# Retention ahead of two feed-forward networks on one core: state products in four quarters of the array, five unit buffers, nine early weight slices

## The chip, the cores and the metric

The kernel runs on one core of one Trainium2 chip. The metric is the device time of one execution in microseconds. Three executions of the kernel before took 1071.54, 1073.75 and 1075.57 us; their median is 1073.75 us.

## What is computed

Retention over 4 sequences of 768 tokens with 8 heads of 64 features, and on its output, 3072 tokens of 512 features, two feed-forward networks of width 2048, all in float32:

```python
for t in range(S):
    state = gamma[None, :, None, None] * state + np.einsum('bhd,bhe->bhde', k[:, :, t], v[:, :, t])
    y[:, :, t] = scale * np.einsum('bhd,bhde->bhe', q[:, :, t], state)
x = np.ascontiguousarray(y.transpose(0, 2, 1, 3)).reshape(B * S, H * D)
h = x @ w_in
x = (h * (1.0 / (1.0 + np.exp(-1.702 * h)))) @ w_out
r = np.maximum(x @ w_in2, 0.0)
out = (r * r) @ w_out2
```

## The kernel before

The work has two parts on PE. The first 106 us are the **retention stage**: 24 units (4 sequences of 6 pieces of 128 tokens), each with all 8 heads. The rest are the two networks, in blocks of tokens, with float32 values split into a high and a low float32r part so that each product takes three matmuls. The first network's first block of 512 tokens (`n == 0` of the loop at line 719) runs in 16 steps `f` of 24 matmuls.

A **unit** is one tile of 128x2048 (1 MB: q and k transposed in pairs of heads, then k and v by tokens). It is loaded by two DMAs on SP's queue (`load_unit`, line 444) into one of `UNITS` buffers. In step `u` of the loop at line 563 the program issues, in this order:

- `scores(u)`: eight matmuls of 64 rows give k times q for each head (line 459, tile `sc`, two banks, two buffers). The two heads of a pair lie in the upper and lower half of the partitions, so they use different row halves of the array. Then v is scaled (`vs`), on POOL for the first six units and each third one (line 478), on ACT otherwise (line 483).
- `split_0()`: for the first four units the output of two steps ago is split into the network's operands, by four casts on ACT (line 494) and four subtractions on DVE (line 495).
- `outputs(u - 1)`: eight matmuls of 64 columns multiply the masked scores `pt` by `vs` into `yp` (line 508); eight of 64x64 outputs add k times v to the sequence's state in PSUM, `dp` (line 518); ACT copies that state to SBUF (line 525), as two blocks of 64x64 per pair on the diagonal of a 128x128 tile whose other blocks were filled with zeros once (line 431); and four matmuls of 128x128 add the state up to the unit before, times q, to `yp` (line 529), in all units but the first of a sequence.
- `cv_step(...)`: on DVE the mask of unit `u` (line 468, `masked`) and the scaling of the output of unit `u - 1` (lines 542, 546, 549, `scaled`), and between them, where `u` is in `CVU`, the conversion of one **weight slice** of the first network. A slice is 512 KB; it is loaded from POOL's queue into one of five `raw` buffers (`cv_load`, line 109), rescaled by two ACT operations (lines 124, 125; `cv_a`, up to two slices ahead), joined by three DVE operations (lines 129, 134, 142), and one step later split by a cast on ACT (line 157) and a subtraction on DVE (line 162). There are 32 slices; those not made in this stage are made in the steps `f` of the first block (lines 608 to 611). `cv["ahead"]` says how many slices may be loaded ahead.
- `load_unit(u + UNITS - 1)` on SP, into the buffer of unit `u - 1`.

Every engine works through its instructions in the order in which the program issued them. SP also lets each DMA wait for the landing of the one eight of its DMAs earlier. Behind the loop the pools of this stage are closed, and the network starts with `up(0, 0)` (line 594).

Of the kernel before, what the change touches and what calls it, by code (L numbers as in the profile page):

```python
# [10 lines left out]
F32 = mybir.dt.float32  # L11
# [19 lines left out]
WA = 8  # L31
LOOK = 2
WARM = 10
UNITS = 4
XHELD = 4
NL = NT // (2 * TB)
NQ = NF // 2
# [4 lines left out]
SLOTS = 8  # L42
EARLY = 2
BG = 4.8
CVU = (6, 8, 10, 12, 14, 16, 18, 20, 21, 22, 23)
RAWS = 5
BGUP = 1.8

# [9 lines left out]
def tile_retention_then_two_ffns(  # L58
# [10 lines left out]
    nc = tc.nc  # L69
    v = nc.vector  # L70
# [13 lines left out]
    xout = {j: keep_p.tile([P, KD, TB], F32, tag=f"xo{j}", name=f"xout{j}") for j in range(XHELD, NT // TB)}  # L84
# [310 lines left out]
    xs = {}  # L395
# [14 lines left out]
    with tc.manual_schedule():  # L410

        with (
# [13 lines left out]
            table_sb = att.tile([P, 1], F32, tag="table", name="table_sb", bufs=1)  # L426
            nc.scalar.activation(out=table_sb, in_=warm_sb[:, 0:1], func=ACTF.Gelu_apprx_sigmoid)

            st_sb = [att.tile([P, NP, P], F32, tag=f"st{i}", name=f"st{i}", bufs=1) for i in range(2)]
            for t in st_sb:  # L430
                nc.gpsimd.memset(t, 0.0)
            hl[0] = hl_tiles(0)
            cv["pool"] = att


            warm = aps.tile([P, 2, NP, P], F32, tag="sc", name="warm")
# [15 lines left out]
            def scores(u):  # L452
                t = units[u]
                qk = t[:, 0:1024].rearrange("p (b n a i) -> p b n a i", b=2, n=2, a=2)
                v = t[:, 1536:2048].rearrange("p (h e) -> p h e", h=H)
                sc = aps.tile([P, 2, NP, P], F32, tag="sc", name=f"sc{u}")
                for p in range(NP):
                    for r in range(2):
                        nc.tensor.matmul(  # L459
                            sc[:, r, p, :],  # L460
                            qk[64 * r:64 * r + 64, p // 2, 1, p % 2, :],
                            qk[64 * r:64 * r + 64, p // 2, 0, p % 2, :],
                            start=True, stop=True,
                        )
                pt = att.tile([P, 2, NP, P], F32, tag="pt", name=f"pt{u}")

                def masked():
                    nc.vector.tensor_tensor(
                        out=pt.rearrange("p r a i -> p (r a) i"),
                        in0=sc.rearrange("p r a i -> p (r a) i"),  # L470
                        in1=mask_sb.unsqueeze(1).to_broadcast([P, H, P]),
                        op=ALU.mult,
                    )

                vs = att.tile([P, H, D], F32, tag="vs", name=f"vs{u}")
                if u < CPB or u % 3 == 0:

                    nc.gpsimd.tensor_tensor(
                        out=vs, in0=v, in1=vtab_sb[:, u % CPB, :].unsqueeze(2).to_broadcast([P, H, D]), op=ALU.mult
                    )  # L480
                else:
                    for h in range(H):
                        nc.scalar.mul(vs[:, h, :], v[:, h, :], vtab_sb[:, u % CPB, h:h + 1])
                pend[u] = (pt, vs)
                return masked

            def split_0():
# [4 lines left out]
                for k in range(KD):  # L492
# [3 lines left out]
                        out=lo[:, cols], in0=xt[:, k, :], in1=hi[:, cols], op=ALU.subtract  # L496
                    )

            def outputs(u):
                t = units.pop(u)  # L500
                pt, vs = pend.pop(u)
                b, c = divmod(u, CPB)
                qk = t[:, 0:1024].rearrange("p (b n a i) -> p b n a i", b=2, n=2, a=2)
                kn = t[:, 1024:1536].rearrange("p (h e) -> p h e", h=H)
                yp = aps.tile([P, NP, P], F32, tag="yp", name=f"yp{u}")
                for p in range(NP):
                    for r in range(2):
                        nc.tensor.matmul(  # L508
                            yp[64 * r:64 * r + 64, p, :], vs[:, 2 * p + r, :], pt[:, r, p, :],
                            start=(p == 0), stop=(c == 0), skip_group_check=True,  # L510
                        )
                dp, st = state.pop(b, (None, None))
                if c == 0:
                    dp = aps.tile([P, 2, NP, D], F32, tag="dp", name=f"dp{b}")
                if c < CPB - 1:
                    for p in range(NP):
                        for r in range(2):
                            nc.tensor.matmul(
                                dp[64 * r:64 * r + 64, 0, p, :], kn[:, 2 * p + r, :], vs[:, 2 * p + r, :],
                                start=(c == 0 and p == 0), stop=(c == CPB - 2), skip_group_check=True,  # L520
                            )
                    ns = st_sb[u % 2]
                    for r in range(2):
                        h = slice(64 * r, 64 * r + 64)
                        nc.scalar.copy(out=ns[h, :, h], in_=dp[h, 0])
                    state[b] = (dp, ns)
                if c > 0:
                    for p in range(NP):
                        nc.tensor.matmul(  # L529
                            yp[:, p, :], st[:, p, :], qk[:, p // 2, 0, p % 2, :],  # L530
                            start=False, stop=True, skip_group_check=True,
                        )
                j, o = divmod(u, UPB)
                cols = slice(o * P, (o + 1) * P)
                if 0 < j < XHELD and o == 0:
                    xs[j] = block_tiles(f"x{j}")

                def scaled():
                    if 0 < j < XHELD:
                        for i in range(2):  # L540
                            pair = slice(2 * i, 2 * i + 2)
                            v.tensor_tensor(
                                out=xs[j][i][:, :, cols], in0=yp[:, pair], in1=ytab_sb[c][:, pair], op=ALU.mult
                            )
                    elif j > 0:
                        v.tensor_tensor(out=xout[j][:, :, cols], in0=yp, in1=ytab_sb[c], op=ALU.mult)
                    else:
                        xt = att.tile([P, NP, P], F32, tag="x0", name=f"x0_{u}")
                        v.tensor_tensor(out=xt, in0=yp, in1=ytab_sb[c], op=ALU.mult)
                        pend["x"] = (xt, cols)  # L550

                return scaled
# [10 lines left out]
            for u in range(NU + 1):  # L563
                masked = scores(u) if u < NU else None
                split_0()
                scaled = outputs(u - 1) if u > 0 else None
                if 0 < u < CPB:
                    for p in range(NP):
                        nc.scalar.mul(ytab_sb[u][:, p, :], ytab_sb[0][:, p, :], ystep_sb[:, u, p:p + 1])
                if u == 16:  # L570
                    cv["ahead"] = RAWS
                cv_step(2 * WA if u in CVU else 0, masked, scaled, u >= 4)
                if u > 0:
                    load_unit(u + UNITS - 1)

# [13 lines left out]
        def up(n, f):  # L589
            hi, lo = weights(f, 0)  # L590
            hp = hp_p.tile([P, TB], F32, tag="h", name=f"h{n}_{f}")
            for k in range(KD):
                xh, xl = hl[n][k]
                nc.tensor.matmul(hp, lo[:, k], xh, start=(k == 0), stop=False)  # L594
                nc.tensor.matmul(hp, hi[:, k], xh, start=False, stop=False)  # L595
                nc.tensor.matmul(hp, hi[:, k], xl, start=False, stop=(k == KD - 1))  # L596
            g = g_p.tile([P, TB], F32, tag="gs", name=f"gs{n}_{f}", bufs=1)
            gh = g_p.tile([P, TB], F32R, tag="gh", name=f"gh{n}_{f}")
            gl = g_p.tile([P, TB], F32R, tag="gl", name=f"gl{n}_{f}")

            nc.scalar.activation(out=g, in_=hp, func=ACTF.Gelu_apprx_sigmoid)  # L601
            nc.scalar.copy(out=gh, in_=g)  # L602
            gs[n, f] = (gh, gl)

            def low():
                v.tensor_tensor(out=gl, in0=g, in1=gh, op=ALU.subtract)  # L606

            if n == 0 and cv["b"] < len(order):
                cv_step(len(order), None, low)
                if f % 2 == 0:  # L610
                    cv_step()
            else:
# [106 lines left out]
        for n in range(NSTD):  # L719
            for f in range(NF):  # L720
# [8 lines left out]
                if n == 0 and f in (2, 3):  # L729
                    j = XHELD + f - 2  # L730
# [273 lines left out]
def _pairs_T(q, k):  # L1004

    a = np.stack([q, k]).reshape(2, B, 2, 2, 2, CPB, P, D)
    return a.transpose(1, 5, 4, 7, 2, 0, 3, 6).reshape(NU, P, 2 * NP * P)


# [55 lines left out]
```

## Time and profile before

| | us |
|---|---|
| median of three runs | 1073.75 |
| the profiled execution | 1076.15 |
| its span, first to last instruction | 1074.4 |
| PE busy in the span | 1052.1 |
| DVE busy | 747.3 |
| ACT busy | 533.2 |
| first matmul of the first network | 106.33 |

The profiled execution is 1.75 us longer than its span. A row of the trace names the line, the engine, the operation and the tiles (out<-in); "idle before" is time in which the engine stood, with what ended it behind an arrow. `PEclk` is the granted share of TensorE's clock, 1.00 for 2.4 GHz and 0.50 for 1.2. In lists of PE each float32 matmul of the retention stage has two records, so eight matmuls read as x16.

### The profile page before, as it was taken

The page shows a single profiled execution, that of the slowest core. Times are in us where ns is not written, and L with a number is a line of the kernel's source. Part 1 is how long each engine was busy: PE and PEld are TensorE (multiplying, and loading weights), DVE is VectorE, ACT ScalarE, POOL GpSimd, SP SyncE. Part 2 cuts the span into 40 slices and gives each one's busy share as a digit, 9 for nine tenths or more (in the row PEclk, how much of TensorE's full clock was granted, in tenths as well). Part 3 has the DMA queues.
Part 4 walks back from the last instruction along what each step waited for, and adds up shares of the span by engine and source line. Part 5 has one row for each costly group of instructions (what it writes and reads, how often), then busy time and mean ns, then how long its engine had stood idle before and what let it go on. Part 6 is the DMA issues. An engine that isn't in the chain of part 4 may idle for free.

```text
span 1074.4 us, 15219 instructions
## 1 busy us (share of the span) xinstructions
PE 1052.1 (98%) x5482; PEld 872.2 (81%) x5482; DVE 747.3 (70%) x1069; ACT 533.2 (50%) x878; POOL 100.7 (9%) x149
## 2 busy tenths in 40 slices
PE   8889999999999999999999999999999999999998
PEld 6778888888888888777888878888888888888886
DVE  4778977888678787946498544789345888345953
ACT  4777765444565657554546333456233455233443
POOL 3111210111011121111000100000100000000000
PEclk8999999999999999999999999999999999999999
DMA  8997686855478688699866786666876666766664
GB/s 272 386 343 271 235 299 226 319 193 195 177 247 266 202 315 290 219 365 355 242 209 193 251 271 195 189 213 212 281 225 191 192 211 231 217 195 195 198 206 165
DMA packets 106652, 259.33 MB, mean 241 GB/s; under 512 B 11217, under 2 KB 11345, under 8 KB 106321
## 3 DMA queue, kind: packets, MB, share of 16 engines
q1 hardware_dynamic: 79088, 156.64, 45.6%
q0 software_dynamic: 22304, 83.89, 22.3%
q10 hardware_dynamic: 5184, 17.83, 4.6%
q8 instruction: 44, 0.72, 0.3%
q14 instruction: 32, 0.25, 0.1%
HBM read 184.91 MB, written 73.40 MB: 240 GB/s over the span
## 4 chain that ended last, share of the span: by engine, by line
PE 82%; DMA 11%; DVE 4%; issue 1%; ACT 1%; POOL 0%; SPq 0%; DVEq 0%; ACTq 0%; POOLq 0%
PE D L768 28%; PE X L768 14%; PE Z L768 7%; DMA unit<-qkv 5%; PE h L595 4%; PE h L594 4%; PE h L596 4%; PE y L627 4%; PE y L626 4%; PE y L625 4%; DMA r<-kw 4%; PE Y L768 4%; PE yp L508 1%; DMA raw<-wout 1%; PE sc L459 1%; PE yp L529 1%
## 5 line engine op out<-in xcount | busy, mean ns | idle before, releaser
L768 PE MATMUL D<-gx,r 128*128 128x512 f32 x1344 | 306.3, 389 | 0.0
L768 PEld LDWEIGHTS D<-gx,r 128*128 128x128 f32 x1344 | 252.1, 188 | 52.9 <-DVE gx L871 0.8
L870 ACT CAST gx<-g 128x1024 fp32r<-128x1024 f32 x112 | 116.6, 1052 | 92.9 <-PE D L768 83.3
L871 DVE TENSOR_TENSOR gx<-g,gx 128x1024 fp32r<-128x1024 f32 x112 | 136.5, 1221 | 36.9 <-ACT gx L870 36.7
L768 PE MATMUL X<-xh,r 128*128 128x512 f32 x512 | 157.9, 390 | 0.2 <-DMA r<-kw 0.2
L789 ACT COPY g<-X 128x512 f32<-128x512 f32 x96 | 56.5, 589 | 186.6 <-PE X L768 186.6
L794 DVE TENSOR_TENSOR g<-Z,g 128x512 f32<-128x512 f32 x64 | 44.2, 691 | 145.6 <-ACT g L789 101.2
L768 PEld LDWEIGHTS X<-xh,r 128*128 128x128 f32 x512 | 95.9, 188 | 21.1 <-issue 1.0
L627 PE MATMUL y<-gl,w 128*128 128x512 f32 x256 | 99.7, 390 | 0.6 <-DVE gl L606 0.6
L594 PE MATMUL h<-hl,w 128*128 128x512 f32 x256 | 99.7, 389 | 0.0
L626 PE MATMUL y<-gh,w 128*128 128x512 f32 x256 | 99.6, 389 | 0.0
L625 PE MATMUL y<-gh,w 128*128 128x512 f32 x256 | 99.6, 389 | 0.0
L768 PE MATMUL X<-xl,r 128*128 128x512 f32 x256 | 99.6, 389 | 0.0
L596 PE MATMUL h<-hl,w 128*128 128x512 f32 x256 | 99.6, 389 | 0.0
L595 PE MATMUL h<-hl,w 128*128 128x512 f32 x256 | 99.6, 389 | 0.0
L768 PE MATMUL Z<-xh,r 128*128 128x512 f32 x256 | 79.2, 391 | 2.6 <-DMA r<-kw 2.0
L602 ACT CAST gh<-gs 128x512 fp32r<-128x512 f32 x64 | 39.8, 622 | 80.2 <-PE y L626 79.6
L606 DVE TENSOR_TENSOR gl<-gs,gh 128x512 fp32r<-128x512 f32 x64 | 44.1, 689 | 46.3 <-ACT gh L602 46.3
L601 ACT ACTIVATE gs<-h 128x512 f32<-128x512 f32 x64 | 38.2, 597 | 50.2 <-PE h L596 44.3
L768 PEld LDWEIGHTS Z<-xh,r 128*128 128x128 f32 x256 | 47.7, 188 | 14.0 <-DVE g L847 1.9
L627 PEld LDWEIGHTS y<-gl,w 128*128 128x128 f32 x256 | 48.1, 188 | 11.2 <-DVE gl L606 1.2
L625 PEld LDWEIGHTS y<-gh,w 128*128 128x128 f32 x256 | 48.1, 188 | 10.0
(96 smaller groups left out, 1572.7 us busy)
## 6 DMA issues: line engine op xcount, KB each, us to landing
r<-kw SPq DMA_DIRECT2D x448, 256.0 KB, 2.9
kw<-wq POOLq DMA_DIRECT2D x32, 896.0 KB, 5.7
unit<-qkv SPq DMA_DIRECT2D x47, 512.0 KB, 8.1
raw<-w POOLq DMA_DIRECT2D x32, 512.0 KB, 6.5
kw<-wh POOLq DMA_DIRECT2D x16, 1024.0 KB, 4.7
kw<-w SPq DMA_DIRECT2D x16, 512.0 KB, 6.7
raw<-win ACTq DMA_DIRECT2D x16, 512.0 KB, 5.6
raw<-wout ACTq DMA_DIRECT2D x16, 512.0 KB, 3.9
```

The source lines that it names most:

```text
L594: nc.tensor.matmul(hp, lo[:, k], xh, start=(k == 0), stop=False)
L595: nc.tensor.matmul(hp, hi[:, k], xh, start=False, stop=False)
L596: nc.tensor.matmul(hp, hi[:, k], xl, start=False, stop=(k == KD - 1))
L606: v.tensor_tensor(out=gl, in0=g, in1=gh, op=ALU.subtract)
L625: nc.tensor.matmul(a, lo[:, e], gh, start=s0, stop=False)
L626: nc.tensor.matmul(a, hi[:, e], gh, start=False, stop=False)
L627: nc.tensor.matmul(a, hi[:, e], gl, start=False, stop=s1)
L768: nc.tensor.matmul(a, w, b, start=start, stop=stop, skip_group_check=True)
L789: nc.scalar.copy(out=t, in_=a)
L794: v.tensor_tensor(out=t, in0=a, in1=t, op=ALU.add)
L870: nc.scalar.copy(out=hi, in_=src)
L871: v.tensor_tensor(out=lo, in0=src, in1=hi, op=ALU.subtract)
```

## The change

- State times q becomes eight matmuls of 64x64 outputs: head `2p` uses row half 0 and column half 0 for an even pair `p`, row half 1 and column half 0 for an odd one; `yp` gets a bank for the even pairs and a bank for the odd ones. q and k of odd pairs are laid out with their halves exchanged by the host. The state is copied as it lies, in one ACT copy, and the zero-filled tiles are gone.
- `yp` now has two tiles of two banks; `sc` has one tile of two banks instead of two such tiles; `dp` is half as wide.
- Five unit buffers instead of four.
- Nine steps convert a slice in the stage instead of eleven: 5, 8, 11, 14, 17, 20, 21, 22, 23. Loads of slices begin in step 2 instead of 4, and the limit of five ahead holds from step 18 instead of 16.
- In the first block of the network the second conversion of a step is made in three of four steps instead of one of two.

```diff
-UNITS = 4
+UNITS = 5
-CVU = (6, 8, 10, 12, 14, 16, 18, 20, 21, 22, 23)
+CVU = (5, 8, 11, 14, 17, 20, 21, 22, 23)
...
-            st_sb = [att.tile([P, NP, P], F32, tag=f"st{i}", name=f"st{i}", bufs=1) for i in range(2)]
-            for t in st_sb:
-                nc.gpsimd.memset(t, 0.0)
...
-                sc = aps.tile([P, 2, NP, P], F32, tag="sc", name=f"sc{u}")
+                sc = aps.tile([P, 2, NP, P], F32, tag="sc", name=f"sc{u}", bufs=1)
...
+            def banked(t):
+                return t.rearrange("p (k b) i -> p b k i", b=2)
...
-                yp = aps.tile([P, NP, P], F32, tag="yp", name=f"yp{u}")
+                yp = aps.tile([P, 2, NP, P], F32, tag="yp", name=f"yp{u}")
                 for p in range(NP):
                     for r in range(2):
                         nc.tensor.matmul(
-                            yp[64 * r:64 * r + 64, p, :], vs[:, 2 * p + r, :], pt[:, r, p, :],
-                            start=(p == 0), stop=(c == 0), skip_group_check=True,
+                            yp[64 * r:64 * r + 64, p % 2, p // 2, :], vs[:, 2 * p + r, :], pt[:, r ^ p % 2, p, :],
+                            start=(p < 2), stop=(c == 0), skip_group_check=True,
                         )
...
-                    dp = aps.tile([P, 2, NP, D], F32, tag="dp", name=f"dp{b}")
+                    dp = aps.tile([P, NP, D], F32, tag="dp", name=f"dp{b}")
...
-                    ns = st_sb[u % 2]
-                    for r in range(2):
-                        h = slice(64 * r, 64 * r + 64)
-                        nc.scalar.copy(out=ns[h, :, h], in_=dp[h, 0])
+                    ns = att.tile([P, NP, D], F32, tag="st", name=f"st{u}")
+                    nc.scalar.copy(out=ns, in_=dp)
                     state[b] = (dp, ns)
                 if c > 0:
                     for p in range(NP):
-                        nc.tensor.matmul(
-                            yp[:, p, :], st[:, p, :], qk[:, p // 2, 0, p % 2, :],
-                            start=False, stop=True, skip_group_check=True,
-                        )
+                        for r in range(2):
+                            a = slice(64 * (r ^ p % 2), 64 * (r ^ p % 2) + 64)
+                            nc.tensor.matmul(
+                                yp[64 * r:64 * r + 64, p % 2, p // 2, :], st[a, p, :], qk[a, p // 2, 0, p % 2, :],
+                                start=False, stop=True, skip_group_check=True,
+                            )
...
-                        v.tensor_tensor(out=xout[j][:, :, cols], in0=yp, in1=ytab_sb[c], op=ALU.mult)
+                        v.tensor_tensor(out=banked(xout[j][:, :, cols]), in0=yp[:, :, 0:2], in1=banked(ytab_sb[c]), op=ALU.mult)
...
-                if u == 16:
+                if u == 18:
                     cv["ahead"] = RAWS
-                cv_step(2 * WA if u in CVU else 0, masked, scaled, u >= 4)
+                cv_step(2 * WA if u in CVU else 0, masked, scaled, u >= 2)
...
-                if f % 2 == 0:
+                if f % 4 < 3:
                     cv_step()
...
+    a = np.stack([a[:, :, :, 0], a[:, :, :, 1, ::-1]], axis=3)
```

How this moves instructions is shown at three places. The first is POOL's queue from unit 2 on, before (`vs_237` is unit 2's scaled v, `vs_343` unit 4's):

```order
L478 TENSOR_TENSOR vs_237<-unit_166,tab_sb 128x512
L478 TENSOR_TENSOR vs_290<-unit_169,tab_sb 128x512
L478 TENSOR_TENSOR vs_343<-unit_224,tab_sb 128x512
L119 DMA raw_383<-w 128x1024
L119 DMA raw_385<-w 128x1024
L478 TENSOR_TENSOR vs_400<-unit_277,tab_sb 128x512
L119 DMA raw_444<-w 128x1024
```

and now (`vs_236` is unit 2's):

```order
L475 TENSOR_TENSOR vs_236<-unit_162,tab_sb 128x512
L119 DMA raw_280<-w 128x1024
L119 DMA raw_282<-w 128x1024
L475 TENSOR_TENSOR vs_297<-unit_165,tab_sb 128x512
L119 DMA raw_343<-w 128x1024
L475 TENSOR_TENSOR vs_358<-unit_168,tab_sb 128x512
L475 TENSOR_TENSOR vs_417<-unit_223,tab_sb 128x512
L119 DMA raw_468<-w 128x1024
```

The first two slice loads stand behind unit 2's scaling instead of unit 4's, and the fourth behind unit 5's.

The second is ACT's queue in steps 3 and 4, before (`ytab_131` is the last operation of step 3, the casts of `x_2` are the first of step 4):

```order
L569 ACTIVATE ytab_131<-ytab_128,tab_sb 128x128 x4
L494 CAST hl_0_142<-x_2_328 128x128
L494 CAST hl_0_143<-x_2_328 128x128
L494 CAST hl_0_144<-x_2_328 128x128
L494 CAST hl_0_145<-x_2_328 128x128
L525 COPY st_139<-dp_206 64x4x64 x2
```

and now:

```order
L570 ACTIVATE ytab_131<-ytab_128,tab_sb 128x128 x4
L124 ACTIVATE raw_280<-raw_280 128x512
L125 ACTIVATE raw_280<-raw_280 128x512
L491 CAST hl_0_138<-x_2_341 128x128
L491 CAST hl_0_139<-x_2_341 128x128
L491 CAST hl_0_140<-x_2_341 128x128
L491 CAST hl_0_141<-x_2_341 128x128
L524 COPY st_385<-dp_205 128x256
```

The first slice's rescaling, which waits for that slice to land, stands ahead of step 4's casts and of the state copy behind them.

The third is one unit on PE with its waits, before (`sc` is the next unit's scores):

```order
L518 MATMUL dp_206<-vs_290,unit_169 64x64 [waits DMAHW2_49,Activation_49]
L518 MATMUL dp_206<-vs_290,unit_169 64x64 x7
L529 MATMUL yp_353<-unit_169,st_138 128x128 x4
L459 MATMUL sc_390<-unit_277 128x128 [waits DMAHW5_49,PE_49]
L459 MATMUL sc_390<-unit_277 128x128 x7
```

and now:

```order
L519 MATMUL dp_205<-vs_297,unit_165 64x64 [waits DMAHW2_49,Activation_49]
L519 MATMUL dp_205<-vs_297,unit_165 64x64 x7
L530 MATMUL yp_368<-unit_165,st_324 64x128 x8
L456 MATMUL sc_407<-unit_223 128x128 [waits DMAHW5_49,DVE_49]
L456 MATMUL sc_407<-unit_223 128x128 x7
```

The state's four products are eight, and the scores wait for the unit's DMA and for DVE (the mask of the unit before).

## Rows read from the trace of the kernel before

**Rows 1.** The page's chain of waits, by line (shares of the span).

```profile
PE D L768 28%; PE X L768 14%; PE Z L768 7%; DMA unit<-qkv 5%; PE h L595 4%; PE h L594 4%; PE h L596 4%; PE y L627 4%; PE y L626 4%; PE y L625 4%; DMA r<-kw 4%; PE Y L768 4%; PE yp L508 1%; DMA raw<-wout 1%; PE sc L459 1%; PE yp L529 1%
```

**Rows 2.** Windows: length, busy us (instructions) by engine, granted clock, DMA share, GB/s.

```profile
12.31:106.33 94.02, 83.59 (x1217) 75.95 (x1217) 70.66 (x116) 67.78 (x207) 19.86 (x27) 0.96 0.90 330
...
120.00:1074.40 954.40, 946.93 (x4165) 780.50 (x4164) 661.79 (x931) 452.17 (x650) 75.94 (x111) 1.00 0.71 234
```

**Rows 3.** Groups by line, PE, 12.3 to 106.33 us: busy, mean ns, idle before.

```profile
L459 PE MATMUL sc<-unit 64*128 64x128 f32 x352 | 26.3, 290 | 9.3 <-DMA unit<-qkv 9.3
```

**Rows 4.** Smaller windows of the retention stage, columns as in rows 2.

```profile
34.00:44.00 10.00, 6.90 (x112) 6.35 (x114) 6.82 (x12) 7.18 (x23) 0.03 (x1) 1.00 1.03 408
...
...
84.00:88.00 4.00, 4.00 (x63) 3.58 (x63) 2.82 (x4) 2.39 (x10) 0.59 (x1) 0.89 0.55 152
16.00:28.00 12.00, 12.00 (x182) 10.95 (x180) 8.18 (x18) 9.73 (x36) 5.59 (x7) 0.97 0.84 277
```

**Rows 5.** Waits of SP's queue, 12 to 93 us: in total, times, longest.

```profile
SPq L450 <- PE yp L529: 50.5, 16, 6.1
SPq L450 <- PE dp L518: 12.1, 4, 5.6
```

**Rows 6.** DVE's timeline, last units: start, length, instruction, idle before.

```profile
90.18 0.69 DVE L162 TENSOR_TENSOR w<-hm,w 128x512 fp32r<-128x512 f32 x1 [2.29 <-ACT w L157]
90.79 0.42 DVE L129 TENSOR_SCALAR hm<-raw 128x512 uint32<-128x512 uint32 x1
91.12 1.22 DVE L468 TENSOR_TENSOR pt<-sc,tab_sb 128x1024 f32<-128x1024 f32 x1
...
94.54 1.22 DVE L468 TENSOR_TENSOR pt<-sc,tab_sb 128x1024 f32<-128x1024 f32 x1
95.67 0.76 DVE L134 SCALAR_TENSOR_TENSOR hm<-raw,hm 128x512 uint32<-128x512 uint32 x1
...
103.03 1.22 DVE L468 TENSOR_TENSOR pt<-sc,tab_sb 128x1024 f32<-128x1024 f32 x1
```

**Rows 7.** PE's timeline, one unit in the middle and the next one's start.

```profile
49.17 0.63 PE L518 MATMUL dp<-vs,unit 128*64 128x64 f32 x16
49.74 1.16 PE L529 MATMUL yp<-unit,st 128*128 128x128 f32 x8
50.83 1.16 PE L459 MATMUL sc<-unit 64*128 64x128 f32 x16
51.92 1.09 PE L508 MATMUL yp<-pt,vs 128*64 128x128 f32 x16
52.84 0.64 PE L518 MATMUL dp<-vs,unit 128*64 128x64 f32 x16
```

**Rows 8.** PE's timeline, the first network's first matmul.

```profile
106.33 0.47 PE L594 MATMUL h<-hl,w 128*128 128x512 f32 x1
```

**Rows 9.** Groups by line: ACT to 106 us, and one of the page.

```profile
L525 ACT COPY st<-dp 64x256 f32<-64x256 f32 x40 | 14.7, 367 | 24.3 <-PE dp L518 23.5
...
L494 ACT CAST hl<-x 128x128 fp32r<-128x128 f32 x16 | 3.5, 290 | 0.0
...
L789 ACT COPY g<-X 128x512 f32<-128x512 f32 x96 | 56.5, 589 | 186.6 <-PE X L768 186.6
```

**Rows 10.** Timelines of POOL and ACT, and DMA issues of 14 to 24 us.

```profile
15.70 1.04 POOL L478 TENSOR_TENSOR vs<-unit,tab_sb 128x512 f32<-128x512 f32 x1 [2.27 <-DMA unit<-qkv]
...
23.24 1.24 POOL L119 DMA_DIRECT2D raw<-w  x2
...
22.99 1.28 ACT L569 ACTIVATE ytab<-ytab,tab_sb 128x128 f32<-128x128 f32 x4
...
raw<-w POOLq DMA_DIRECT2D x2, 512.0 KB, 8.8
```

**Rows 11.** PE's timeline and windows (columns as in rows 2), 80 to 85 us.

```profile
80.09 1.16 PE L459 MATMUL sc<-unit 64*128 64x128 f32 x16 [2.69 <-DMA unit<-qkv]
...
81.47:84.88 3.41, 3.41 (x26) 2.86 (x22) 2.80 (x3) 0.00 (x0) 1.31 (x2) 0.50 0.71 284
```

More of the change, by code (lines that the diff above doesn't have):

```diff
@@ L427, in tile_retention_then_two_ffns @@
             nc.scalar.activation(out=table_sb, in_=warm_sb[:, 0:1], func=ACTF.Gelu_apprx_sigmoid)
-            st_sb = [att.tile([P, NP, P], F32, tag=f"st{i}", name=f"st{i}", bufs=1) for i in range(2)]
-            for t in st_sb:
-                nc.gpsimd.memset(t, 0.0)
             hl[0] = hl_tiles(0)
             cv["pool"] = att
-            warm = aps.tile([P, 2, NP, P], F32, tag="sc", name="warm")
+            warm = aps.tile([P, 2, NP, P], F32, tag="sc", name="warm", bufs=1)
             for i in range(WARM):
@@ L455, in scores @@
                 v = t[:, 1536:2048].rearrange("p (h e) -> p h e", h=H)
-                sc = aps.tile([P, 2, NP, P], F32, tag="sc", name=f"sc{u}")
+                sc = aps.tile([P, 2, NP, P], F32, tag="sc", name=f"sc{u}", bufs=1)
                 for p in range(NP):
-                    for r in range(2):
+                    for a in range(2):
                         nc.tensor.matmul(
-                            sc[:, r, p, :],
-                            qk[64 * r:64 * r + 64, p // 2, 1, p % 2, :],
-                            qk[64 * r:64 * r + 64, p // 2, 0, p % 2, :],
+                            sc[:, a, p, :],
+                            qk[64 * a:64 * a + 64, p // 2, 1, p % 2, :],
+                            qk[64 * a:64 * a + 64, p // 2, 0, p % 2, :],
                             start=True, stop=True,
@@ L513, in outputs @@
                 if c == 0:
-                    dp = aps.tile([P, 2, NP, D], F32, tag="dp", name=f"dp{b}")
+                    dp = aps.tile([P, NP, D], F32, tag="dp", name=f"dp{b}")
                 if c < CPB - 1:
                     for p in range(NP):
-                        for r in range(2):
+                        for a in range(2):
+                            h = 2 * p + (a ^ p % 2)
                             nc.tensor.matmul(
-                                dp[64 * r:64 * r + 64, 0, p, :], kn[:, 2 * p + r, :], vs[:, 2 * p + r, :],
+                                dp[64 * a:64 * a + 64, p, :], kn[:, h, :], vs[:, h, :],
                                 start=(c == 0 and p == 0), stop=(c == CPB - 2), skip_group_check=True,
                             )
-                    ns = st_sb[u % 2]
-                    for r in range(2):
-                        h = slice(64 * r, 64 * r + 64)
-                        nc.scalar.copy(out=ns[h, :, h], in_=dp[h, 0])
+                    ns = att.tile([P, NP, D], F32, tag="st", name=f"st{u}")
+                    nc.scalar.copy(out=ns, in_=dp)
                     state[b] = (dp, ns)
@@ L542, in scaled @@
                             v.tensor_tensor(
-                                out=xs[j][i][:, :, cols], in0=yp[:, pair], in1=ytab_sb[c][:, pair], op=ALU.mult
+                                out=xs[j][i][:, :, cols], in0=yp[:, :, i], in1=ytab_sb[c][:, pair], op=ALU.mult
                             )
                     elif j > 0:
-                        v.tensor_tensor(out=xout[j][:, :, cols], in0=yp, in1=ytab_sb[c], op=ALU.mult)
+                        v.tensor_tensor(out=banked(xout[j][:, :, cols]), in0=yp[:, :, 0:2], in1=banked(ytab_sb[c]), op=ALU.mult)
                     else:
                         xt = att.tile([P, NP, P], F32, tag="x0", name=f"x0_{u}")
-                        v.tensor_tensor(out=xt, in0=yp, in1=ytab_sb[c], op=ALU.mult)
+                        v.tensor_tensor(out=banked(xt), in0=yp[:, :, 0:2], in1=banked(ytab_sb[c]), op=ALU.mult)
                         pend["x"] = (xt, cols)
```

## The prediction

> **What bounds the kernel now.** The page's chain of waits comes first [rows 1]: most of it is the two feed-forward networks on PE. Only one entry names a transfer ahead of them, `unit<-qkv` with 5% of the span: units of q, k and v for the retention stage. The windows table places it [rows 2]. From 120 us to the end PE is busy 946.93 of 954.40 us, so nothing can be won there but by cutting matmuls, and the change cuts none. In the retention stage, 12.31 to 106.33 us, PE is busy 83.59 of 94.02 us and idle for 10.4; DVE is busy 70.66, ACT 67.78, and the DMA engines run at a share of 0.90 and 330 GB/s. Nobody is full on average, DMA is nearest. In the table of lines [rows 3] PE's idle time stands on one line: 9.3 us before the scores, released by the unit's DMA.
>
> Why the transfers are late shows in two views. The smaller windows [rows 4] have stretches at 408 GB/s and a share of 1.03, and others at 0.84 or, around 84 us, 0.55. And SP's own waits [rows 5] say that it held loads back for 50.5 + 12.1 us until PE let go of a unit's buffer: 20 waits, 3.1 us each. So the stage alternates: DMA waits for a free buffer, then PE waits for DMA.
>
> The end of the stage is bounded by something else. In DVE's timeline [rows 6] the masks of the last three units begin at 94.54 to 103.03: 4.2 us a unit, DVE without a gap, because units 20 to 23 each carry a weight slice (four more DVE operations) on top of mask and scaling. PE's unit takes 3.67 us [rows 7]. The first network's first matmul starts at 106.33 [rows 8], 3.3 us after the last mask began.
>
> **The change, part by part.**
>
> *State times q.* Now four matmuls of 128x128 take 1.09 us a unit (50.83 less 49.74) [rows 7], twenty units. Eight quarters of 64x64 are nowhere in this trace. Nearest are the eight 64-row scores, two at a time, 1.09 us (51.92 less 50.83), and the eight 64-column products `yp`, 0.92 us (52.84 less 51.92) [rows 7]. Four at a time would be 0.46 to 0.55. Bounds: 0.46, half of `yp`, and 8 x 0.27 = 2.18, twice the scores, if no two quarters overlap. I take 0.55, since row halves overlap and column halves overlap in two separate rows: 20 x 0.54 = 10.8 us of PE, which leaves 72.8 us. PE is not the one that is full, so this is slack: it lets go of buffers 0.54 us sooner and shortens the last unit by 0.5 us.
>
> The Trainium skill's page "TensorEngine Tiling (Array Packing)", Restrictions and Gotchas, says that different row tiles cannot access one PSUM bank at the same time. By it the two quarters of a pair of heads, which share a bank and come from different row halves, go one after the other; no row here shows two row halves on one bank. The second rival is what it would make of the time.
>
> *State copy.* Two copies of 64x256 at 367 ns become one of 128x256. Between the 128x128 cast (290 ns) and the 128x512 copy (589 ns) [rows 9] it takes about 0.39 us: 0.35 us less on ACT, twenty times. ACT is ahead of DVE in the last units (its cast released DVE at 90.18 after 2.29 us [rows 6]), so this helps there, by at most that 2.29 us. The two zero fills on POOL stand ahead of its wait for the first unit and go: worth 0.
>
> *Single score tile.* The scores of a unit now wait for the mask of the one before, where they waited for the mask two units back (PE's own order covered that). Queued behind them on PE are the products of the unit before, which need that same mask anyway. Between a unit's scores and the next ones lie 0.92 + 0.57 + 0.55 us of PE (`yp`, `dp`, state [rows 7]); the mask takes 1.22 us [rows 6]. Hidden, unless DVE is late; then up to 1.1 us a unit (the scores lose their head start), which in the last units lies beside DVE's own 4.2 us. I take 0. The scaling reads two banks in place of one with as many elements: 0.
>
> *Fifth buffer.* A load is issued one unit (3.1 to 3.7 us) sooner, which is the mean wait on SP. The share of 0.90 leaves 0.10 x 94 = 9.4 us of DMA time unused. Not all comes back, since SP also lets each load wait for the landing of the one eight loads earlier. Bounds 0 and 9.4; I take half, 4.7 us, as gaps like the one at 84 us lie behind a whole chain of late work.
>
> *Nine slices.* Two slices of 512 KB fewer are loaded before the last unit: 1.05 MB at 330/0.90 = 367 GB/s is 2.9 us of DMA. The same two go into the first network's block 0, on DVE and ACT at 2.57 us (0.42 to 0.76 us for each of four operations [rows 6], with their overlap) a slice. There the change makes 7 slices in 4 blocks of 24 matmuls: 7 x 2.57 + 4 x 0.69 (a low part, an operation like the first of [rows 6]) = 20.8 us of DVE against 4 x 5.5 = 22.0 us of PE (954.40 us for 4165 matmuls [rows 2]). It fits, with some 1 us to spare; if not, PE would wait for a low part that it needs two blocks later. Cost 0, at worst 1 us.
>
> *Slices loaded two units sooner.* POOL issues the first two behind unit 2's scaling (15.70 to 16.74) instead of unit 4's, about 16.8 us instead of 23.24 [rows 10], and ACT meets the first rescaling two steps sooner, ahead of the casts for unit 2's tokens. The first slices took 8.8 us to land [rows 10], so 25 to 26 us; ACT reaches the rescaling after the `ytab` operations that now end at 24.3 [rows 10], and with the faster PE and copies some 1 us sooner. ACT, and behind it casts, masks and, by the single score tile, PE stand for 1 to 3 us. The transfers go on meanwhile, into five buffers, so I put 1 us on the path (bounds 0 and 3).
>
> *Sum.* -4.7 -2.9 +1 = -6.6 us, at best -9.4 -2.9 = -12.3, at least -2.9 + 3 = 0. The last units check it: units that land 6 us sooner bring unit 20's mask from 91.12 to about 84 (the 2.29 us wait gone partly), then three units of 4.2 us, the mask's 1.2 and PE's last 1.5 (`yp` and state) give 99.3 for the first matmul of the network, against 106.33. Beyond it everything moves along. The profiled execution took 1076.15 us, 2.40 over the median 1073.75; -6.6 on the median gives **1067.2 us**.
>
> **Rivals.**
>
> *Transfers stay the bound.* If the new buffer only lengthens the queue, two slices' 2.9 us remain: 1070.9. For it: 34 to 44 us, where share and rate are at their highest and PE still waits. Against it: the 62.6 us in which SP stood. 0.20, ACT's early wait included.
>
> *Quarters of one bank take turns*: the phase stays near 1.09 us and PE's work at 83.6 us. With transfers sooner PE has 94.0 - 83.6 = 10.4 us to give, and a unit's buffer is let go later, so a third of the gaps comes back: -3.1 -2.9 +1 = -5.0, 1068.8. 0.12. The rule of the Trainium skill's page cited above would have it so.
>
> *Quarters do not overlap at all* (slower). If each quarter waits for the last, the phase is 2.18 us, PE's work 83.6 + 20 x 1.09 = 105.4, and the stage ends 11.4 us later than now even with no other wait: 1085. It decides from 10.4/20 = 0.52 us above 1.09, so from 1.6 us a unit. For it: nothing shown; against: both halves overlap singly. 0.05.
>
> *DMA runs through* (more): all gaps filled, and DVE's last units alone bound the end: -10 or so, 1063.8. 0.15.
>
> *The clock.* After the wait that ends at 80.09 the granted clock is at 1.2 GHz, half, from 81.47 to 84.88 [rows 11]. PE had stood for 2.69 us before 80.09. With less PE work such stretches may be more; each costs up to half its 3.4 us of PE, of which there is now plenty. No case of its own, 1 us of the range.
>
> **How the numbers follow.** The forecast (-4.5 to -9, so 1064.8 to 1069.3) has 0.48. The filled case below it and the transfer case above it, with 1 us each for the clock and the measurement, give the range **1063 to 1072**; it leaves out the slower rival, the outer bounds of the sum (-12.3 and 0) and what lies between, some 0.15. A measurement of this kernel can tell 0.5%, 5.4 us. Faster by more: most of the forecast (0.36), the filled case (0.15), a little of the turn-taking one: **0.55**. Within: **0.40**. Slower: **0.05**.
>
> **What would show it.** The state products at 0.55 us a unit between `dp` and the next scores; PE's idle time before the scores down from 9.3 to about 5 us; the first network's first matmul near 99.7 us instead of 106.33; DMA share of the stage at 0.95; the masks of the last units still 4.2 us apart. A first matmul after 104 us, or a state phase above 1.1 us, makes it wrong.

## The result, and the profile after

Five executions of the changed kernel took 1058.28 to 1060.56 us, median 1059.31; five of the kernel before, taken beside them, have the median 1072.69. The ratio is 0.9868 [0.9849, 0.9887], which is 14.2 us or 1.3%; the two medians lie 13.4 us apart. The forecast was 1067.2 in a range of 1063 to 1072, so the direction was right, the forecast gain of 6.6 us was half of what came, and the result lies below the range.

The profiled execution took 1059.31 us, its span 1057.5. The first network starts at 91.22 us instead of 106.33 [rows 8], 15.1 us sooner, and what lies behind it takes 966.3 us (1057.5 less 91.22) against 968.1 before. So nearly the whole gain was made in the retention stage. (The profiled execution of before lies 3.5 us over the median of its five runs, which is why 15.1 + 1.8 is more than 13.4; in a middling execution the network would start at about 103, an estimate.)

The chain of waits of the changed kernel, by line:

```profile
PE D L769 29%; PE X L769 16%; PE Z L769 8%; PE h L595 6%; PE y L628 6%; PE y L626 5%; PE y L627 5%; PE h L596 5%; PE h L597 5%; PE Y L769 4%; DMA r<-kw 2%; DMA unit<-qkv 2%; PE yp L508 1%; PE sc L456 1%; DMA raw<-w 1%; DVE pt L465 1%
```

The units' DMAs have 2% of it instead of 5% [rows 1]. The windows of the changed kernel (length, busy us and instructions of PE, PEld, DVE, ACT, POOL, granted clock, DMA share, GB/s):

```profile
12.00:91.22 79.22, 73.37 (x1376) 64.46 (x1376) 64.03 (x107) 55.10 (x181) 20.09 (x24) 0.96 0.97 378
...
40.00:80.00 40.00, 39.45 (x774) 34.65 (x770) 34.62 (x55) 26.35 (x89) 8.59 (x11) 1.00 1.02 397
...
27.00:31.90 4.90, 4.08 (x48) 3.85 (x48) 4.18 (x9) 2.66 (x9) 1.58 (x2) 0.65 1.03 410
```

Against [rows 2] the stage has 10.2 us less of PE's work (73.37 for 83.59), and PE stands for 5.9 us instead of 10.4. From 40 to 80 us PE and the transfers are both full: 39.45 of 40 us and 397 GB/s. PE's groups by line and its waits, 12 to 91 us, and SP's waits:

```profile
L456 PE MATMUL sc<-unit 64*128 64x128 f32 x352 | 25.9, 287 | 4.9 <-DVE pt L465 3.9 <-DMA unit<-qkv 0.9
```

```profile
SPq L447 <- PE yp L530: 35.6, 15, 5.7
SPq L447 <- PE dp L519: 8.7, 4, 3.7
```

The 9.3 us that the scores waited for a unit [rows 3] are 0.9. In their place stand 3.9 us of a wait that the kernel before did not have, for the mask. SP is held for 44.3 us instead of 62.6 [rows 5]. PE's timeline at two places and at the start of the network:

```profile
24.48 0.67 PE L530 MATMUL yp<-unit,st 64*64 64x128 f32 x16
...
27.82 1.50 PE L456 MATMUL sc<-unit 64*128 64x128 f32 x16 [2.68 <-DVE pt L465]
29.26 1.97 PE L508 MATMUL yp<-pt,vs 128*64 128x128 f32 x16
...
41.23 1.16 PE L456 MATMUL sc<-unit 64*128 64x128 f32 x16
...
43.81 0.67 PE L530 MATMUL yp<-unit,st 64*64 64x128 f32 x16
44.41 1.16 PE L456 MATMUL sc<-unit 64*128 64x128 f32 x16
...
91.22 0.50 PE L595 MATMUL h<-hl,w 128*128 128x512 f32 x1
```

The state products take 0.60 us from start to start (44.41 less 43.81), where the 128x128 ones took 1.09 [rows 7]. At 27.82 PE has stood for 2.68 us behind a mask and then works slower: products that take 1.09 us elsewhere take 1.97, and the window of 27.0 to 31.9 us has a granted clock of 0.65, a mix of 1.2 and 2.4 GHz. Where the wait comes from is read from ACT and DVE, whose lists also show the last units:

```profile
24.30 0.68 ACT L124 ACTIVATE raw<-raw 128x512 f32<-128x512 f32 x1 [1.28 <-DMA raw<-w]
...
25.43 0.88 ACT L491 CAST hl<-x 128x128 fp32r<-128x128 f32 x4
```

```profile
25.74 0.89 DVE L492 TENSOR_TENSOR hl<-x,hl 128x128 fp32r<-128x128 f32 x4 [3.01 <-ACT hl L491]
26.56 1.21 DVE L465 TENSOR_TENSOR pt<-sc,tab_sb 128x1024 f32<-128x1024 f32 x1
...
76.07 1.23 DVE L465 TENSOR_TENSOR pt<-sc,tab_sb 128x1024 f32<-128x1024 f32 x1 [0.33 <-PE sc L456]
...
79.49 1.22 DVE L465 TENSOR_TENSOR pt<-sc,tab_sb 128x1024 f32<-128x1024 f32 x1
...
83.89 1.22 DVE L465 TENSOR_TENSOR pt<-sc,tab_sb 128x1024 f32<-128x1024 f32 x1
...
88.24 1.22 DVE L465 TENSOR_TENSOR pt<-sc,tab_sb 128x1024 f32<-128x1024 f32 x1
```

ACT reaches the first slice's rescaling and waits 1.28 us for it to land; the casts stand behind the two operations of that rescaling, DVE's subtraction waits 3.01 us for the casts, the mask stands behind that, and PE's next scores wait for the mask. The masks of the last three units lie 4.4 us apart, as they lay 4.2 apart before [rows 6]; the network follows the last one by 2.98 us.

### The profile page after: what moved, and what is told of

Same layout as the page of the kernel before. It is cut to its first block, busy times and chain, and to the rows that moved or that the text cites. A ratio compares the mean times of both kernels' runs of the same rounds, so it can differ in the third digit from the quotient of the medians.

```text
span 1057.5 us, 15484 instructions
## 1 busy us (share of the span) xinstructions
PE 1040.0 (98%) x5642; PEld 859.7 (81%) x5642; DVE 746.1 (71%) x1069; ACT 523.5 (49%) x858; POOL 101.5 (10%) x147
## 4 chain that ended last, share of the span: by engine, by line
PE 92%; DMA 5%; DVE 1%; ACT 1%; SPq 0%; issue 0%; POOL 0%; ACTq 0%; POOLq 0%; DVEq 0%
PE D L769 29%; PE X L769 16%; PE Z L769 8%; PE h L595 6%; PE y L628 6%; PE y L626 5%; PE y L627 5%; PE h L596 5%; PE h L597 5%; PE Y L769 4%; DMA r<-kw 2%; DMA unit<-qkv 2%; PE yp L508 1%; PE sc L456 1%; DMA raw<-w 1%; DVE pt L465 1%
## 5 line engine op out<-in xcount | busy, mean ns | idle before, releaser
L628 PEld LDWEIGHTS y<-gl,w 128*128 128x128 f32 x256 | 48.1, 188 | 10.4 <-DVE gl L607 0.4
L595 PEld LDWEIGHTS h<-hl,w 128*128 128x128 f32 x256 | 48.1, 188 | 10.1 <-issue 0.2
```

The source lines that it names most:

```text
L628: nc.tensor.matmul(a, hi[:, e], gl, start=False, stop=s1)
```

## Experiments

The question is where the 7 to 8 us come from that the sum did not have (13.4 or 14.2 us for its 6.6). All edits are made on the kernel before or on the changed one, as each says. "Wait" is PE's idle time before the scores in the profiled execution, "start" the first network matmul there. The ratios are to the kernel before, and times in us worked out from them are shares of its 1072.4.

| run | ratio [95%] | start, us | wait: unit's DMA / mask, us |
|---|---|---|---|
| before | 1 | 106.33 | 9.3 / 0 |
| quarters_alone | 0.9973 [0.9960, 0.9985] | 99.77 | 7.8 / 6.6 |
| buffer_alone | 0.9925 [0.9903, 0.9946] | 97.44 | 0.9 / 0 |
| slices_alone | 0.9996 [0.9975, 1.0017] | 97.70 | 4.7 / 0 |
| quarters_and_slices | 0.9964 [0.9948, 0.9980] | 95.18 | 5.8 / 4.4 |
| buffer_and_slices | 0.9930 [0.9908, 0.9952] | 95.50 | 0.1 in all |
| quarters_and_buffer | 0.9904 [0.9879, 0.9929] | 94.78 | 0 / 10.7 |
| the change | 0.9868 [0.9849, 0.9887] | 91.22 | 0.9 / 3.9 |

Where the network starts is not the whole time. The profiled executions of quarters_alone, slices_alone and quarters_and_slices lie 1.6, 5.1 and 4.3 us under the medians of their runs, those of before and buffer_alone 3.5 and 2.4 us over them, and by the ratios the first three gained less than their starts say; the ratios decide. One part of this scatter is seen at the start of the stage. From 11 to 15 us the granted clock was 0.50 in before and 1.00 in slices_alone, though its edit acts only from step 2 on; it was 1.00 in later_rescale below and 0.57 in the change:

```profile
11.00:15.00 4.00, 3.01 (x36) 2.89 (x38) 1.35 (x2) 0.13 (x1) 1.98 (x2) 0.57 1.02 409
```

So a start is a reading of one execution, from which 2 us and more can be scatter.

**The changed kernel without the fifth buffer and with the old slices** (state in quarters, one copy, single score tile):

```diff
-UNITS = 5
+UNITS = 4
-CVU = (5, 8, 11, 14, 17, 20, 21, 22, 23)
+CVU = (6, 8, 10, 12, 14, 16, 18, 20, 21, 22, 23)
...
-                if u == 18:
+                if u == 16:
...
-                cv_step(2 * WA if u in CVU else 0, masked, scaled, u >= 2)
+                cv_step(2 * WA if u in CVU else 0, masked, scaled, u >= 4)
...
-                if f % 4 < 3:
+                if f % 2 == 0:
```

> Only the state products in quarters (with the single score tile and the single state copy that go with them); four buffers and the eleven slices as before. Theory A, that of the prediction (PE's time is slack; the transfers and the last units decide): -1 us, first matmul of the network at about 105.5 us. Theory B (PE's time is on the path because it lets go of the buffers, and a buffer released sooner is a load issued sooner): 20 x 0.49 us off PE's part of each round trip, -6 to -10 us, first matmul at 96 to 100. Theory C (only buffer and quarters together fill the transfer gaps): -2 to -4 us.

Measured: 2.9 us faster (0.0027 of 1072.4), as theory C has it; the start of 99.77 us is in theory B's band, in an execution 1.6 us under the median. PE's groups by line:

```profile
L456 PE MATMUL sc<-unit 64*128 64x128 f32 x352 | 25.9, 287 | 14.5 <-DMA unit<-qkv 7.8 <-DVE pt L465 6.6
```

PE works some 10 us less, and in the profiled execution half of that turns into waiting: it stands for 14.5 us before the scores instead of 9.3, about half of it for transfers that are late nearly as before (7.8 us for 9.3), half for the mask, which the single score tile has put there.

**The kernel before with the fifth buffer alone:**

```diff
-UNITS = 4
+UNITS = 5
```

> The kernel before with five unit buffers instead of four, nothing else. Theory A: half the transfer gaps, -4.7 us, first matmul at 101.6. Theory B: PE's unit of 3.67 us then bounds the middle; -5 to -8, since PE's 83.6 us of work leave at most 10.4. Theory C: -2 to -4, as a unit still occupies its buffer 3.67 us.

Measured: 8.0 us faster, more than theory A's half of the gaps. The window of the stage and PE's wait before the scores:

```profile
12.00:97.44 85.44, 82.16 (x1217) 74.75 (x1217) 69.45 (x117) 68.18 (x208) 20.04 (x28) 0.97 0.95 361
```

```profile
L459 PE MATMUL sc<-unit 64*128 64x128 f32 x352 | 26.3, 291 | 0.9 <-DMA unit<-qkv 0.9
```

The buffer alone takes the wait for units from 9.3 to 0.9 us, not to half. PE is then busy for 82.16 of 85.44 us: with the old state products PE's own 3.67 us a unit [rows 7] is the next limit, and PE stands for only 3.3 us more.

**The kernel before with the new slices alone** (CVU, the limit at `u == 18`, loads from `u >= 2`, `f % 4 < 3`, as in the change's diff):

> The kernel before with the new slice schedule (nine steps, loads from step 2, five ahead from step 18, three of four steps in block 0). Theory A: 2.9 us less transfer, 1 us given back by ACT's early wait: -1.9 us, first matmul at 104.4. Theories B and C: -2 to -4, as fewer slices compete with the units; the early wait of ACT is there in the trace, one to three us long.

Measured: the interval runs from 2.7 us faster to 1.8 us slower. The sum's own value for it, -2.9 + 1 = -1.9, lies inside; so does no change at all. The run does not decide between them. ACT's early wait for the first slice is in its trace, 0.7 us long.

**Pairs of the three parts.** Each is the changed kernel or the one before with the edits above combined.

> The change with four buffers instead of five. Theory A: -2.9 +1 -1 = -3 us, first matmul at 103. Theory B: most of the gain is there without the fifth buffer, -10 to -13, first matmul at 94 to 96. Theory C: -4 to -7, the rest needs the buffer.

> The change without the quarters: the kernel before with five buffers and the new slice schedule, state by four 128x128 products. Theory A: nearly all of the gain, -13 us measured less 1: first matmul at 92 to 93. Theory B: PE's 83.6 us of work plus the early wait bound the stage: first matmul at 97 to 99, -8 to -9 us. Theory C: the same place or later, -6 to -9.

> The change with the slice schedule of before (eleven steps, loads from step 4). Two slices more, 1.05 MB, are moved before the last unit and ACT's early wait is not there. If the transfers bound the stage now (DMA share 1.01 at 390 to 404 GB/s from 40 to 80 us in the changed kernel): 1.05 MB / 0.4 = 2.6 us later, less the early wait of about 3 us that the transfers hide: first matmul at 93 to 95, -11 to -12 us. If DVE's last units bound it: as the change, 91 to 92.

Measured: -3.9, -7.5 and -10.3 us. With quarters and slices the transfers stay late (5.8 us), so without the buffer the rest gives little. Buffer and slices together show PE as the limit, in windows:

```profile
12.00:95.50 83.50, 80.04 (x1201) 72.69 (x1197) 68.16 (x107) 64.27 (x201) 18.17 (x24) 0.98 0.95 356
...
40.00:80.00 40.00, 40.00 (x617) 36.39 (x617) 33.90 (x50) 29.41 (x94) 6.87 (x9) 1.00 0.97 353
```

From 40 to 80 us PE does not stand at all, and the transfers fall to 353 GB/s; SP is held for 51.5 us until PE lets go of a buffer. The two slices less give nothing here that the intervals show (0.9925 and 0.9930). From this kernel to the change only the state products and what goes with them (copy, score tile, `yp` on two banks) differ, and that is 0.9930 to 0.9868: 6.6 us, in intervals that don't meet. With quarters and buffer, and eleven slices, the start of 94.78 us falls in the band that was expected if transfers bound the stage, but the scores never wait for a unit there; the wait is the mask's. PE's groups by line:

```profile
L456 PE MATMUL sc<-unit 64*128 64x128 f32 x352 | 25.8, 286 | 10.7 <-DVE pt L465 10.7
```

DVE converts slices between masks, and with one score tile each conversion can hold PE. What holds it is seen in this kernel's chain of waits, by start and length:

```profile
49.06 0.37 ACT st L524
49.43 0.59 ACT raw L124
50.02 0.55 ACT raw L125
50.57 0.51 ACT w L157
...
51.11 0.69 DVE w L162
51.80 0.34 DVE hm L129
52.13 1.14 DVE pt L465
...
53.32 1.16 PE sc L456 x16
```

PE's state products release the state copy on ACT; behind it stand two rescalings and the cast of the slice's high part; DVE's subtraction waits for that cast (7 times in the stage, 7.0 us), the mask stands behind the subtraction, and the scores wait for the mask. From 39.30 to 81.28 us this chain comes round every 7.0 us, for two units, and no transfer is in it. So it is the round through three engines, none of them full, that bounds the middle of this kernel, where PE's own unit in the change takes 3.18 us (44.41 less 41.23). With a slice in every third step DVE waits for that cast for 1.5 us instead of 7.0, and the mask's wait is 3.9 us, 2.7 of it the early one at 27.82. The slices are then worth 3.9 us by the ratios (2.3 by the medians), in intervals that overlap. By the waits they pay through the order of ACT's and DVE's queues, and not by the 2.9 us of transfer that the sum gave them; but the transfers of quarters_and_buffer are near their best rate too (398 GB/s from 40 to 80 us), so it is not shown that fewer bytes alone would give nothing.

**Do two row halves on one bank take turns?** The changed kernel with both heads of each pair on the diagonal quarters, so that two quarters at most can run at a time:

```diff
-  vs[:, 2 * p + r, :], pt[:, r ^ p % 2, p, :],
+  vs[:, 2 * p + r, :], pt[:, r, p, :],
...
-  h = 2 * p + (a ^ p % 2)
+  h = 2 * p + a
...
-  a = slice(64 * (r ^ p % 2), 64 * (r ^ p % 2) + 64)
+  a = slice(64 * r, 64 * r + 64)
```

(and the host's layout without the exchange).

> The change with every pair of heads in the same two quarters (upper left, lower right), so that only two quarters can be at work at once, both writing to one bank from different row halves. If two such quarters overlap, the phase is 1.0 to 1.1 us a unit instead of 0.60, and PE's work is 9 to 10 us more: first matmul at 92 to 95 if that is slack, 97 or later if PE is on the path. If different row halves cannot write one bank at once: about 2.2 us a unit, first matmul beyond 115.

Measured: 0.9919 [0.9894, 0.9944], start 96.38 us. PE's timeline, then the windows:

```profile
45.18 1.09 PE L530 MATMUL yp<-unit,st 64*64 64x128 f32 x16
46.20 1.16 PE L456 MATMUL sc<-unit 64*128 64x128 f32 x16
```

```profile
12.00:96.38 84.38, 81.91 (x1377) 73.36 (x1377) 69.42 (x109) 56.21 (x182) 19.29 (x26) 0.96 0.95 354
```

Eight quarters take 1.02 us with two at a time (46.20 less 45.18), and 0.60 in the change. If quarters of one bank took turns, the change too could have no more than two in work, one on each bank. Two at a time make four turns of eight quarters; this run's 1.02 us is four turns, or five if the rule held in it too and its first and last quarter stood alone, so the change could not be under 0.82 us, an estimate from the 1.02. It takes 0.60, so they overlap. By the Trainium skill's "TensorEngine Tiling (Array Packing)", Restrictions and Gotchas, different row tiles cannot access one PSUM bank at the same time; for these fp32 matmuls, which write different partition halves of the bank, the trace shows otherwise. The run is also the cleanest price of PE's work: 20 x 0.42 = 8.4 us more of it, with buffers, slices and score tile as in the change, cost 5.5 us by the ratios (0.9868 to 0.9919, intervals that don't meet) and 3.7 by the medians, with PE busy for 81.91 of 84.38 us. The start lies between the two bands that were expected, in an execution 2.5 us over the median.

**The early rescaling.** The changed kernel with loads from step 2 on, but no rescaling on ACT before step 4:

```diff
+    late = [False]
...
-        if cv["pool"] is not None and limit is not None:
+        if cv["pool"] is not None and limit is not None and late[0]:
...
+                late[0] = u >= 4
```

> The change with ACT's first rescaling of a slice left out of steps 2 and 3, so that it comes behind the casts of step 4. In the changed kernel PE waited 2.68 us for a mask behind ACT's wait for the first slice, and the granted clock fell behind it. If the transfers hide that: same time, first matmul at 91. If it is on the path: 2 to 4 us sooner, first matmul at 87 to 89.

Measured: 1055.70 to 1058.15 us, median 1056.42, ratio 0.9851 [0.9829, 0.9873], start 87.55. The window of the stage:

```profile
12.00:87.55 75.55, 69.08 (x1344) 60.38 (x1345) 64.96 (x107) 55.25 (x181) 18.30 (x23) 1.00 0.99 393
```

The wait at 27.82 us is now 1.40 us long and the clock is full throughout (1.00). Against the change's 1058.28 to 1060.56 that is 2.9 us by the medians, in ranges that don't meet (1.8 by the ratios, whose intervals do). The start is 3.7 us sooner, but that is no price of the rescaling: of the two profiled executions this one began step 2's scores at 12.44 us and the change's at 14.75, before the edit acts, with the clock at 1.00 there against 0.57.

**The single score tile by itself**, in the kernel before and in that with the fifth buffer:

```diff
-                sc = aps.tile([P, 2, NP, P], F32, tag="sc", name=f"sc{u}")
+                sc = aps.tile([P, 2, NP, P], F32, tag="sc", name=f"sc{u}", bufs=1)
```

(and the same for `warm`, its first user).

> The kernel before with one score tile instead of two, nothing else: a unit's scores wait for the mask of the unit before. If the term is 0, as the prediction had it (PE's order covers the wait), the time is that of before and no wait of the scores for a mask shows. If the waits of 6.6 and 10.7 us that the scores have for masks in the runs with quarters and eleven slices come from the single tile alone: 3 to 6 us of such waits here too, some of it in place of the wait for the unit's DMA, +1 to +3 us.

> Five buffers and one score tile, state by four 128x128 products, eleven slices. Against the five buffers alone (-8 us): if the single tile costs only where PE is ahead of DVE, PE's longer unit keeps it hidden and the time is the same, with less than 3 us of waits for masks. If it costs wherever a slice is converted (eleven times 0.5 to 1 us): 5 us or more of such waits and -3 to -5 us against before in place of -8.

Measured: 1.0006 [0.9990, 1.0022] and 0.9952 [0.9934, 0.9971]. PE's groups by line, in the first and in the second:

```profile
L459 PE MATMUL sc<-unit 64*128 64x128 f32 x352 | 26.9, 294 | 9.9 <-DVE pt L468 4.8 <-DMA unit<-qkv 3.9 <-DVE hm L142 0.8
```

```profile
L459 PE MATMUL sc<-unit 64*128 64x128 f32 x352 | 25.6, 285 | 7.1 <-DVE pt L468 6.3 <-DMA unit<-qkv 0.6
```

While the transfers are late the mask's wait only takes the place of theirs, and the time stays. Once the buffer is there it stands alone: 6.3 us, and the gain falls from 8.0 to 5.1 us (the two intervals overlap, so the 2.9 us are not clear of noise; the wait itself is in the trace).

**Fewer and other slices**, both on the kernel with the later rescaling:

```diff
-CVU = (5, 8, 11, 14, 17, 20, 21, 22, 23)
+CVU = (5, 8, 11, 14, 17, 20, 22)
```

> The version with the later rescaling and seven steps with a slice instead of nine (5, 8, 11, 14, 17, 20, 22). DVE is then without a gap only in two of the last four units: 2 x 2.57 us less there, and 1 MB less is loaded before the end. If DVE's last units bound the end: first matmul of the network 3 to 5 us sooner than 87.55. If the last unit's landing does (83.38): 1 to 2 us sooner. In block 0 DVE has 7 slices in 4 steps for two steps longer; if that holds PE up, low parts are waited for there and the rest takes longer than 966 us.

```diff
-CVU = (5, 8, 11, 14, 17, 20, 21, 22, 23)
+CVU = (5, 7, 9, 11, 13, 15, 17, 19, 21)
```

> The version with the later rescaling and nine slices at every other step (5 to 21) instead of four of them in the last four units. The last two units have no slice: DVE's last stretch is 2 x 2.57 us shorter, but two slices more are loaded ahead of the last units. If DVE's last units bound the end: first matmul at 84 to 86. If the transfers do: at 88 to 90, 1 to 2 us later than 87.55.

Measured: 1055.08 us, 0.9842 [0.9823, 0.9861], start 86.64; and 1059.55 us, 0.9882 [0.9862, 0.9902], start 91.36. Nine slices spread evenly are worse than nine crowded at the end, by 3.1 us of the medians, in intervals that overlap, and later than either expectation had it. The mask's waits rise from 4.2 to 7.0 us, and DVE's for ACT's casts from 1.5 to 5.5: a slice in every other step brings the round of quarters_and_buffer back. PE's groups by line with the later rescaling and in the spread kernel:

```profile
L457 PE MATMUL sc<-unit 64*128 64x128 f32 x352 | 25.6, 284 | 5.7 <-DVE pt L466 4.2 <-DMA unit<-qkv 1.4
...
L457 PE MATMUL sc<-unit 64*128 64x128 f32 x352 | 26.0, 288 | 8.2 <-DVE pt L466 7.0 <-DMA unit<-qkv 1.1
```

With seven slices the last unit carries none, and the start is only 0.9 us sooner, 3.4 us behind the landing of the last unit (83.26 us), nearer to what was expected if that landing bounds the end. Seven slices with the later rescaling are the best version run, though not clearly apart from later rescaling alone.

## Why the prediction was right and wrong

**The parts don't add.** Each part alone, and what is lost when it alone is left out of the change, in us by the ratios:

| part | alone | added to the other two |
|---|---|---|
| quarters, copy, single score tile | -2.9 | -6.6 |
| fifth buffer | -8.0 | -10.3 |
| nine slices | -0.4 | -3.9 |

The three alone make -11.3, the change -14.2. The sum gave 0, -4.7 and -1.9. The -3.9 stands on intervals that overlap, the -6.6 and the -10.3 on intervals that don't meet.

Without the quarters the sum came out nearly right: buffer_and_slices measured -7.5 for its -6.6. That was luck in part, since the buffer gave more than its term and the slices nothing beside it that shows. What the forecast lacks is nearly all in the term that it put at 0.

*Quarters.* This is the step that failed: "PE is not the one that is full, so this is slack". It was slack as long as the transfers were late. The same sum then removed half of that lateness, and its next question had to be whose work comes next; it was PE's, as buffer_and_slices shows. The working would have been short: 12.3 us before the stage plus 83.6 of PE's work is 95.9, and that kernel's network starts at 95.50 (so close by some luck: its PE works for 80.04 us and stands for 3.5). The phase was put at 0.55 us and measured 0.60; what was wrong is its worth, 0 for 6.6 us, and the diagonal run bears it out, with 5.5 us for PE's work alone.

*Fifth buffer.* The mechanism (a load one unit sooner) was right; the size, half of 9.4, was taken from the DMA engines' busy share of 0.90. A share of 0.90 here was not 0.90 of the best rate. By bytes, the stage moved 94.02 us x 330 GB/s = 31.0 MB, which at the 408 GB/s of [rows 4] is 76.0 us: by this estimate 18 us of gaps and not 9.4. The changed kernel moves 79.22 x 378 = 29.9 MB, less by the two slices, and holds 397 GB/s for 40 us. So the outer bound of -12.3 us was itself too near, and the landing of the last unit went from 99.25 to 87.04 us.

*Single score tile.* "Hidden, unless DVE is late" was the right condition, and the 0 was not: DVE is late where a slice's cast on ACT comes late. [Rows 6] had a sign of it, DVE's 2.29 us of waiting for that cast. The cost, some 3 us with the buffer and not clear of noise, is paid inside the quarters' net 6.6.

*Early rescaling.* Right in mechanism, place and time: landing forecast at 25 to 26 us, ACT's wait seen until 24.30. Put at 1 us, it measured 1.8 by the ratios and 2.9 by the medians, within its bounds of 0 to 3; the half-clock stretch behind it is part of that, and a different clock at the start of the stage may be part of it too.

*Nine slices.* The 2.9 us of transfers were not what counted. By themselves they measured 0.4 us, with the interval over both values; in the change 3.9 us, not clear of noise, with 3.9 us of waits for masks in place of 10.7. The half of the term that moved two slices to the network held: its first block shows no wait for a low part.

*State copy, last units.* The copy took 369 ns against 0.39 us. The last masks are 4.4 us apart, DVE without a gap, as forecast. The check by them gave 99.3 because it let unit 20's mask come at 84 us; in the changed kernel that mask starts at 76.07.

*Rivals.* Of them "DMA runs through" (0.15) came nearest: gaps nearly all filled, DVE's last units at the end. Its own -10 us was limited by the same 9.4 us. That transfers stay the bound is out by the 0.9 us that the scores still wait for them, though they stay close: the changed kernel's chain of waits leaves PE for a unit's transfer from 72.78 to 83.12 us and reaches the last mask through ACT and DVE; that quarters take turns, and that they don't overlap, by the phase of 0.60 us. The clock, "1 us of the range", was at half in two stretches of the stage: among the first units, as in the kernel before (0.57 and 0.50 from 11 to 15 us), and behind the wait of 2.68 us, which belongs to the early rescaling's price.

## What to carry to other kernels

A part that works on a resource that is not full has no fixed worth: after the fullest resource has been relieved, add up the next one's work in the stage (here 83.6 us of PE) and ask whether the new time is already at that floor. Then follow the round from engine to engine as well: with the buffer, the quarters and eleven slices neither PE, ACT nor DVE was full, and a chain of 7.0 us for two units held all three. Size the gaps of transfers by bytes at the best rate that the trace shows, not by busy share. And a buffer given up to make room costs where its consumer is late, which shows only once the wait that covered it is gone.

## What was not expected of the hardware

Eight 64x64 fp32 products of 128 columns took 0.60 us in four quarters and 1.02 us in two diagonal ones, against 1.09 us for four 128x128 ones that do the same sums, half of it with zeros: the gain is all in the four at a time. Two queues together held 397 GB/s for 40 us of the retention stage in the change, and 407 with the later rescaling. And one wait of 2.68 us on PE was followed by work at half clock, so that its price was more than its length: the products behind it took 1.97 us for 1.09.
